# Seven products of 2x2 blocks for eight in the second layer's output sums

## The chip, the cores and the metric

The kernel runs on one NeuronCore of a Trainium2 chip. The metric is the device time of one execution in microseconds (us). The kernel before took 1028.25 us, the median of three runs (1027.79 to 1028.84).

## The reference, cut to what matters

Block-causal attention gives a matrix of 2304 tokens by 512 features; two feed-forward layers follow, the second of which is what the change is about.

```python
def reference(**kwargs):
    ...
    x = np.ascontiguousarray(attn_out.transpose(0, 2, 1, 3)).reshape(B * S, H * D)
    x = _moe_ref(x=x, **moe_kwargs)
    return _moe2_ref(x=x, **moe2_kwargs)

def _moe2_ref(x, w_in, w_out):          # x (2304, 512), w_in (512, 2048), w_out (2048, 512)
    h = x @ w_in
    g = np.maximum(0.01 * h, h)
    return (g @ w_out).astype(np.float32)
```

## The kernel before, in words

**Numbers in two parts.** TensorE multiplies a reduced float format (float32r). So that the result is exact enough, each operand is kept as a high part and a low part (the rest), and each product is three matmuls: high by high, high by low, low by high. The names follow this: `gh` and `gl` are the high and low part of an activation tile, and index 0 or 1 of a weight tile `w` is its high or low part.

**Tiling of the feed-forward layers.** `BLOCKS` (L34) cuts the 2304 tokens of each layer into blocks. In the second layer they are four of 512 tokens and one of 256. The 2048 hidden features are 16 chunks of 128 (`NFC`), the 512 input features four of 128 (`NKC`). `moe_block` (L596) goes over the chunks of a block. The first product of a chunk is 12 matmuls (4 input chunks by 3) into a PSUM bank (L618); a block of 256 tokens puts two chunks into one bank (24 matmuls of 256 columns). ACT and DVE then make the activation: ACT scales the bank by 0.01 (L632), DVE takes the maximum (L634), ACT writes `gh` (L636) and DVE `gl` (L637). The second product has the activation as the stationary operand, 128 tokens of it at a time, and a row of 512 outputs as the moving one (L660): four token groups by three matmuls of 512 columns for a chunk of a 512-token block. It adds up over all 16 chunks in one bank for each token group. At a block's end ACT and DVE copy the banks out (L688, L690) and DMAs write them to `out` (L691).

**Order of the work.** All instructions are entered into a planner (`Plan`) with an estimated cost and a due time (`prio`); a list scheduler then writes out one order for each engine (PE, ACT, DVE, POOL) and for SP's queue, which issues all DMAs. On the chip each engine goes through its own list strictly in turn. In the second layer PE's order is: first product of chunk n+1, second product of chunk n, first product of chunk n+2, and so on. So ACT and DVE have the time of a second product (of the chunk before) and of a first product (of the chunk behind) to make one chunk's activation.

**Buffers.** The weights of the second layer, all 16 chunks in two parts, stay in SBUF (`W`, tiles `w`), converted from 64-bit numbers while the first layer's last block runs (`w_float`, `w_hi`, `w_lo`, L323 being the low parts). The input of a block comes from DRAM (`x2d`) into one of two SBUF areas (`xa`, `xb`; `xbuf`, `moe_load`, L593).

Of the kernel before, what the change touches and what calls it, by code (L numbers as in the profile page):

```python
# [9 lines left out]
F32 = mybir.dt.float32  # L10
# [21 lines left out]


BLOCKS = ([(256 * i, 256) for i in range(5)] + [(1280, 512), (1792, 512)],  # L34
          [(0, 512), (512, 512), (1024, 512), (1536, 512), (2048, 256)])
N_WARM = 10

W1_LO = ("dve", "pool")
# [161 lines left out]
def fused_kernel(ctx, tc, qk, v, w1, w2, out):  # L200
# [3 lines left out]
    def bc(ap):  # L204
        return ap.bitcast(F32)
# [14 lines left out]
    x2d = dr.tile([128, 2, NKC, NTOK], F32, tag="x2d", name="x2d")  # L220
    xa = const.tile([128, 4096], F32R, name="xa")


    def pe(cost, prio, fn, r, w):
        plan.op("PE", cost, prio, fn, r, w)

    def act(cols, prio, fn, r, w, sb=False, extra=0):
        plan.op("ACT", (93 if sb else 51) + 0.833 * cols + extra, prio, fn, r, w)

    def dve(cols, prio, fn, r, w, rate=1.042, fixed=68, port=False):  # L230
        plan.op("DVE", fixed + rate * cols, prio, fn, r, w, port)
# [4 lines left out]
    def dma(nbytes, prio, fn, r, w):  # L236
        plan.op("SP", nbytes / 330.0, prio, fn, r, w)
# [38 lines left out]
    def at(ar, shape, dtype, tag, name, bufs=1):  # L276
        return Buf(plan, (id(ar), tag), bufs,
                   lambda: ar.get().tile(shape, dtype, tag=tag, name=name, bufs=bufs), ar)

    def pt(pool_, shape, dtype, tag, name, bufs):  # L280
        return Buf(plan, (id(pool_), tag), bufs, lambda: pool_.tile(shape, dtype, tag=tag, name=name, bufs=bufs))

    def small(tag, name):
        return pt(st, [128, 4], F32, tag, name, 4)

# [6 lines left out]
    def bank(i):  # L292

        ar = None if i in (4, 5) else ps_d if phase["late"] else ps_c
        return Bank(plan, (i,), lambda: banks[i], ar)

    def xbuf(i):

        if i < 2:
            return Bank(plan, (f"x{i}",), lambda: xa[:, 2048 * i:2048 * i + 2048].rearrange("p (c k t) -> p c k t", c=2, k=NKC))  # L300
        if i == 2:
            return Bank(plan, ("x0", "x1"), lambda: xa.rearrange("p (c k t) -> p c k t", c=2, k=NKC))
        return at(rest, [128, 2, NKC, 512], F32R, "xb", f"xb{i}", 1)


    W = {}
# [274 lines left out]

    def moe_load(layer, i, prio):
        t0, tb = BLOCKS[layer][i]
        x = XB[layer, i] = xbuf(i % 2 if tb < 384 and layer == 0 else (8 - i if i > 4 else i % 2) if layer == 0 else 3 - i % 2)
        if (layer, i) == (0, 0):
            return
        src = (x1d, x2d)[layer]
        name = ("x1d", "x2d")[layer]
        for k in range(NKC):
            have = [q for _, q, wr in plan.regions.get(f"{name}{k}", []) if wr]  # L590
            assert all(any(q[0] <= x < q[1] for q in have) for x in range(t0, t0 + tb, 64)), (layer, i, k)
        for c in range(2):
            dma(512 * tb * 4, prio, lambda c=c: nc.sync.dma_start(bc(x.get()[:, c, :, 0:tb]), src[:, c, :, t0:t0 + tb]),  # L593
                [(f"{name}{k}", (t0, t0 + tb)) for k in range(NKC)], [(x, (4 * c, 4 * c + 4))])
# [98 lines left out]

    EVAC = {"a": ("act", "dve"), "b": ("act", "dve", "act")}
    NP = NKC

# [77 lines left out]
    for fc in range(NFC):  # L776
# [3 lines left out]
        for half in range(2):  # L780
# [2 lines left out]
            src, view = w_float(g - 60, 1, fc, half, hs, WF[fc])  # L783
            w_hi(g - 20, 1, fc, half, src, view, True)
            w_lo(g - 20, 1, fc, half, src, view, True, W2_LO[half])
    for i, (_, tb) in enumerate(BLOCKS[1]):
        if i + 1 < len(BLOCKS[1]):
            moe_load(1, i + 1, t - 20)
        moe_block(1, i, t, 5.5 * tb / 512, hb, [2, 3, 0, 1])
        t += 88 * tb / 512  # L790
    plan.schedule()
    stack["sb"].close()
    for x in ("ps2", "ps"):
# [41 lines left out]
```

## Time and profile before

| what | us |
|---|---|
| median of the three runs | 1028.25 |
| the profiled execution: its time | 1028.8 |
| the profiled execution: span from the first to the last instruction | 1027.0 |
| PE busy / weight loads (PEld) busy | 1003.9 / 832.0 |
| DVE, ACT, POOL busy | 460.4, 443.0, 209.7 |
| second layer, first block (first product of its first chunk to that of the next block) | 617.1 to 706.8 |
| second layer, from there to PE's last matmul | 706.8 to 1023.15 |

The profiled execution's time is 1.8 us longer than its span; that part lies outside the instructions. In the profile, PE is the matmul unit and PEld the loading of stationary operands, which overlaps with it. A matmul's own duration (395 ns at 512 columns) contains waiting in the pipeline, so the pace of PE is read from the distance between starts. A stretch in the chain of waits is written as start, length and what it was; "x12" are twelve instructions in a row. DMA is the share of the core's 16 DMA engines that is busy.

### The profile page before, as it was taken

Reading aid. Unit: us, or ns where it says so; the run is one execution under the profiler, and the core shown is the slowest. Engines: PE = TensorE matmul, PEld = TensorE weight load, DVE = VectorE, ACT = ScalarE, POOL = GpSimd, SP = SyncE. Lnnn points to the kernel's source line nnn. Section 1 sums busy time; section 2 is a strip of 40 time slices with the busy share of each in tenths; the row PEclk is TensorE's granted clock in tenths of the full one; section 3 lists DMA queues with packets and bytes.
Section 4 is the critical chain, followed back from the end, with each engine's and each line's share of the span. In section 5 each row is a group of like instructions: output and inputs, shape, how many; then the busy total and the mean of one; then the engine's idle time right before and its main releaser. Section 6 shows DMA issues by size and latency. Waiting matters only on the chain.

```text
span 1027.0 us, 15314 instructions
## 1 busy us (share of the span) xinstructions
PE 1003.9 (98%) x5908; PEld 832.0 (81%) x5908; DVE 460.4 (45%) x800; ACT 443.0 (43%) x1001; POOL 209.7 (20%) x374
## 2 busy tenths in 40 slices
PE   7798999999999999999999999999999999999998
PEld 4487888888888888988887888888888888888897
DVE  5887755454545444344237994223222222322222
ACT  5776756455555454344346763222222222221221
POOL 6755523233222221111005651000000000000000
PEclk8898999999999999999999999999999999999999
DMA  7765533232342132263034643003000200200010
GB/s 248 218 200 171 176 109 110 92 122 86 117 155 90 48 103 69 93 229 120 1 131 143 198 134 153 1 1 123 0 1 24 99 1 1 82 0 1 1 42 21
DMA packets 51208, 95.35 MB, mean 93 GB/s; under 512 B 4800, under 2 KB 28352, under 8 KB 51136
## 3 DMA queue, kind: packets, MB, share of 16 engines
q1 hardware_dynamic: 51136, 94.39, 28.1%
q8 instruction: 46, 0.75, 0.3%
q14 instruction: 26, 0.21, 0.1%
HBM read 71.83 MB, written 22.54 MB: 92 GB/s over the span
## 4 chain that ended last, share of the span: by engine, by line
PE 93%; DVE 2%; ACT 2%; DMA 1%; POOL 1%; issue 1%; SPq 0%; ACTq 0%; DVEq 0%; POOLq 0%
PE bank L618 40%; PE bank L660 20%; PE bank L653 19%; PE slot L545 5%; PE slot L561 5%; PE slot L485 3%; PE slot L500 1%; DMA wraw<-w 1%; ACT pb L407 1%; POOL pb L418 0%; ACT pa L407 0%; POOL pa L418 0%; ACT bank L347 0%; DVE nmb L400 0%; DVE gl L637 0%
## 5 line engine op out<-in xcount | busy, mean ns | idle before, releaser
L618 PE MATMUL bank<-xa,w 128*128 128x256 f32 (+1 forms) x1536 | 279.7, 330 | 4.9 <-DVE gl L637 4.3
L618 PEld LDWEIGHTS bank<-xa,w 128*128 128x128 f32 x1536 | 230.5, 191 | 43.2 <-issue 11.1
L653 PE MATMUL bank<-gh,w 128*128 128x256 f32 (+1 forms) x896 | 186.1, 318 | 0.0
L660 PE MATMUL bank<-w,gh 128*128 128x512 f32 x576 | 180.8, 395 | 0.0
L618 PE MATMUL bank<-xb,w 128*128 128x512 f32 (+1 forms) x768 | 166.0, 366 | 0.0
L634 DVE TENSOR_TENSOR bank<-bank,g 128x512 f32<-128x512 f32 x72 | 50.4, 700 | 246.9 <-ACT g L632 246.9
L618 PEld LDWEIGHTS bank<-xb,w 128*128 128x128 f32 x768 | 132.1, 188 | 26.4
L653 PEld LDWEIGHTS bank<-gh,w 128*128 128x128 f32 x896 | 134.8, 188 | 22.8 <-issue 11.0
L632 ACT ACTIVATE g<-bank 128x512 f32<-128x512 f32 x72 | 43.1, 598 | 253.0 <-PE bank L618 253.0
L637 DVE TENSOR_TENSOR gl<-bank,gh 128x512 fp32r<-128x512 f32 x144 | 99.2, 689 | 70.3 <-ACT gh L636 69.9
L660 PEld LDWEIGHTS bank<-w,gh 128*128 128x128 f32 x576 | 107.6, 188 | 25.4
L636 ACT ACTIVATE gh<-bank 128x512 fp32r<-128x512 f32 x144 | 86.1, 598 | 91.8 <-DVE bank L634 50.1
L653 PE MATMUL bank<-gl,w 128*128 128x256 f32 (+1 forms) x448 | 114.4, 314 | 0.0
L660 PE MATMUL bank<-w,gl 128*128 128x512 f32 x288 | 113.6, 394 | 0.0
L629 DVE SCALAR_TENSOR_TENSOR bank<-bank,g 128x512 f32<-128x512 f32 x72 | 50.2, 698 | 89.2 <-ACT g L628 89.2
L626 ACT ACTIVATE g<-bank 128x512 f32<-128x512 f32 x72 | 43.1, 598 | 87.5 <-PE bank L618 87.2
L653 PEld LDWEIGHTS bank<-gl,w 128*128 128x128 f32 x448 | 73.2, 188 | 5.8
L418 POOL TENSOR_SCALAR pb<-pb,rsb 128x448 f32<-128x448 f32 (+1 forms) x64 | 45.1, 713 | 113.9 <-DVE rsb L413 112.4
L660 PEld LDWEIGHTS bank<-w,gl 128*128 128x128 f32 x288 | 54.1, 188 | 13.0
L407 ACT ACTIVATE pb<-slot,nmb 128x448 f32<-128x448 f32 (+1 forms) x64 | 43.5, 684 | 34.4 <-DVE nmb L400 33.2
L418 POOL TENSOR_SCALAR pa<-pa,rsa 64x64 f32<-64x64 f32 (+2 forms) x96 | 40.1, 434 | 82.5 <-DVE rsa L413 82.3
L407 ACT ACTIVATE pa<-slot,nma 128x64 f32<-128x64 f32 (+2 forms) x96 | 39.4, 422 | 24.6 <-DVE nma L400 23.3
(77 smaller groups left out, 965.5 us busy)
## 6 DMA issues: line engine op xcount, KB each, us to landing
wraw<-w SPq DMA_DIRECT2D x54, 512.0 KB, 4.2
x2d<-yt SPq DMA_DIRECT2D x36, 256.0 KB, 2.5
qkb<-qk SPq DMA_DIRECT2D x16, 416.0 KB, 3.2
qka<-qk SPq DMA_DIRECT2D x16, 320.0 KB, 3.4
more_raw<-w SPq DMA_DIRECT2D x10, 512.0 KB, 4.9
vb<-v SPq DMA_DIRECT2D x16, 320.0 KB, 2.9
out<-yo SPq DMA_DIRECT2D x18, 256.0 KB, 2.1
x1d<-xpb SPq DMA_DIRECT2D x16, 256.0 KB, 2.9
```

The source lines that it names most:

```text
L407: act(keys, prio, lambda view=view, probs=probs, k=k, i=i: nc.scalar.activation(probs[k](), view()[:, k], AF.Exp, bias=nm.get()[:, i:i + 1 ...
L418: pool(keys, prio, lambda probs=probs, k=k, i=i, rows=rows: nc.gpsimd.tensor_scalar(probs[k]()[0:rows], probs[k]()[0:rows], rs.get()[0:row ...
L545: nc.tensor.transpose(s.get()[:, hd, o:o + 128], pr.get()[:, hd, a:a + 128], ident.get())
L561: nc.tensor.matmul(s.get()[64 * hd:64 * hd + 64, 0, q0:q0 + m], lhsT=vt.get()[:, j, 64 * hd:64 * hd + 64], rhs=pts[i].get()[:, hd, o:o + m ...
L618: nc.tensor.matmul(ps.get()[:, j * tb:(j + 1) * tb], lhsT=win(layer, fc, p, kc), rhs=xt.get()[:, x, kc, 0:tb], start=(k == 0 and kc == 0 a ...
L626: act(nw, pv, lambda ps=ps, gt=gt: nc.scalar.activation(gt.get()[:, 0:nw], ps.get()[:, 0:nw], AF.Relu, bias=0.5, scale=0.5), [ps], [gt])
L629: dve(nw, pv, lambda ps=ps, gt=gt: nc.vector.scalar_tensor_tensor(ps.get()[:, 0:nw], ps.get()[:, 0:nw], 1.0, gt.get()[:, 0:nw], op0=ALU.ma ...
L634: dve(nw, pv, lambda ps=ps, gt=gt: nc.vector.tensor_tensor(ps.get()[:, 0:nw], ps.get()[:, 0:nw], gt.get()[:, 0:nw], op=ALU.max), [ps, gt], ...
L636: act(nw, pv, lambda ps=ps, gh=gh: nc.scalar.activation(gh.get()[:, 0:nw], ps.get()[:, 0:nw], AF.Copy), [ps], [gh])
L637: dve(nw, pv, lambda ps=ps, gh=gh, gl=gl: nc.vector.tensor_tensor(gl.get()[:, 0:nw], ps.get()[:, 0:nw], bc(gh.get()[:, 0:nw]), op=ALU.subt ...
L653: nc.tensor.matmul(y[o].get()[:, e * tb:(e + 1) * tb], lhsT=wout(0, fc, p)[:, ec * 128:ec * 128 + 128], rhs=x.get()[:, j * tb:(j + 1) * tb ...
L660: nc.tensor.matmul(y[o].get(), lhsT=x.get()[:, j * tb + o * 128:j * tb + o * 128 + 128], rhs=wout(1, fc, p), start=(fc == 0 and k == 0), s ...
```

## The change

From the second block of the second layer on, tokens are taken in blocks of 256, and two hidden chunks (a pair, 8 pairs) are worked on at a time. The second product of a pair is then a product of 2x2 blocks: on one side two token groups of 128 by two chunks, on the other two chunks by two halves of 256 outputs. The plain way takes eight block products (24 matmuls of 256 columns with the three parts); the changed kernel takes seven (21), with sums and differences of blocks on both sides and seven sums at the end (the scheme of Strassen and Winograd).

- `combine_weights` makes the weight side once for each pair: three combined blocks, which go in two parts to DRAM (`tsd`) because SBUF has no room, and a fourth that is written over the second half of the even chunk's `w`. This is planned beside the first block (still `moe_block`, 512 tokens).
- `moe_seven` takes the place of `moe_block` for the seven blocks of 256. It loads a pair's three combined blocks from `tsd` into one half of `xb` (L773), makes the activation into `e` (L776, L777), four sums and differences of 128 columns (L781), and the high and low parts of all (`ea` L779, L783; `gh`, `gl` L785, L786). The second product is four groups of matmuls on four banks (L816).
- At a block's end one ACT copy and seven DVE sums of 256 columns (L828, L835, L837) make the outputs in place of the copies.

The diff, cut to its core:

```diff
 BLOCKS = ([(256 * i, 256) for i in range(5)] + [(1280, 512), (1792, 512)],
-          [(0, 512), (512, 512), (1024, 512), (1536, 512), (2048, 256)])
+          [(0, 512)] + [(256 * i, 256) for i in range(2, 9)])
...
+    def combine_weights(p, prio):
...
+        for i, w in enumerate((wa, wb)):
+            dve(512, prio, lambda i=i, w=w: nc.vector.tensor_tensor(
+                b(2 * i, 2), bc(w.get()[:, 0, 512:1024]), bc(w.get()[:, 1, 512:1024]), op=ALU.add),
...
+            dve(256, prio, lambda o=o, x=x, y=y: nc.vector.tensor_tensor(t(o), x(), y(), op=ALU.subtract), r, [(tt, (o, o + 1))], port=True)
+        act(256, prio, lambda: nc.scalar.activation(wa.get()[:, 0, 768:1024], t(3), AF.Copy), [(tt, (3, 4))], [(wa, (2, 3))], sb=True)
...
+        act(768, prio, lambda: nc.scalar.activation(b(0, 3).bitcast(F32R), t(0, 3), AF.Copy), [(tt, (0, 3))], [(bb, (0, 3))], sb=True)
...
+            dma(393216, prio, lambda c=c, v=v: nc.sync.dma_start(tsd[:, p, c], v(0, 3)), [(x, (0, 3))], [("tsd", (2 * p + c, 2 * p + c + 1))])
+
+    def moe_seven(i, p0, dp, hbanks, ybanks):
...
+                for j in range(2):
+                    fc = 2 * p + j
+                    for k, (c, x) in enumerate(((0, 0), (1, 0), (0, 1))):
...
+                                nc.tensor.matmul(ps.get()[:, j * 256:(j + 1) * 256], lhsT=win(1, fc, c, kc),
...
+                dma(786432, pr - 4, lambda p=p, tt=tt: nc.sync.dma_start(bc(tt.get()), tsd[:, p].rearrange("p c (i n) -> p c i n", i=3)),
+                    [("tsd", (2 * p, 2 * p + 2))], [tt])
+                pv = pr - 8
+                act(512, pv, lambda ps=ps, e=e: nc.scalar.activation(e.get()[:, 512:1024], ps.get(), AF.Copy, scale=0.01), [ps], [(e, (4, 8))])
+                dve(512, pv, lambda ps=ps, e=e: nc.vector.tensor_tensor(e.get()[:, 0:512], ps.get(), e.get()[:, 512:1024], op=ALU.max),
+                    [ps, (e, (4, 8))], [(e, (0, 4))])
+                act(384, pv, lambda ah=ah, e=e: nc.scalar.activation(ah(0), e.get()[:, 128:512], AF.Copy), [(e, (1, 4))], [(ea, (0, 1))], sb=True)
+                for o, a, b, op in ((4, 0, 2, ALU.add), (5, 4, 1, ALU.subtract), (6, 1, 0, ALU.subtract), (7, 3, 5, ALU.subtract)):
+                    dve(128, pv, lambda at_=at_, o=o, a=a, b=b, op=op: nc.vector.tensor_tensor(at_(o), at_(a), at_(b), op=op),
...
+                act(512, pv, lambda sh=sh, e=e: nc.scalar.activation(sh.get(), e.get()[:, 512:1024], AF.Copy), [(e, (4, 8))], [sh], sb=True)
...
+                for o, prods in enumerate((((av(0), bv(0, 0)), (av(2), bv(1, 0))),
+                                           ((sv(2), tv(2)), (sv(3), tv(3))),
+                                           ((av(1), tv(4)), (sv(1), t1)),
+                                           ((sv(4), bv(1, 1)),))):
...
+                            for k, (ca, cb_) in enumerate(((0, 0), (0, 1), (1, 0))):
+                                nc.tensor.matmul(m[o].get()[:, 256 * z:256 * z + 256], lhsT=a(ca), rhs=b(cb_),
...
-    for i, (_, tb) in enumerate(BLOCKS[1]):
+    moe_load(1, 1, t - 20)
+    moe_block(1, 0, t, 5.5, hb, [2, 3, 0, 1])
+    for p in range(NFC // 2):
+        combine_weights(p, t + 11 * p + 12)
+    t += 88
+    yb = [6, 7, 2, 3, 0, 1]
+    for i in range(1, len(BLOCKS[1])):
         if i + 1 < len(BLOCKS[1]):
             moe_load(1, i + 1, t - 20)
-        moe_block(1, i, t, 5.5 * tb / 512, hb, [2, 3, 0, 1])
-        t += 88 * tb / 512
+        moe_seven(i, t, 5.4, hb, yb)
+        t += 43.2
```

How the rows of three engines change (lines of the changed kernel stand four or more below those of the kernel before):

PE, the middle of a block of the second layer. `w_4` to `w_13` are weight chunks, `gh_1_3` the activation of block 1, chunk 3 (before) or pair 4 (changed). Before, two chunks of 512 tokens:

```order
L618 MATMUL bank_77<-xa,w_4_5956 128x512 x12
L660 MATMUL bank_5133<-w_3_5905,gh_1_3_7120 128x512 [waits Activation_49]
L660 MATMUL bank_5133<-w_3_5905,gh_1_3_7120 128x512
L660 MATMUL bank_5133<-w_3_5905,gl_1_3_7125 128x512 [waits DVE_49]
L660 MATMUL bank_5134<-w_3_5905,gh_1_3_7120 128x512 x2
L660 MATMUL bank_5134<-w_3_5905,gl_1_3_7125 128x512
...
L618 MATMUL bank_78<-xa,w_5_6008 128x512 x12
```

Now one pair of 256 tokens:

```order
L751 MATMUL bank_78<-xa,w_10_6268 128x256 x12
L751 MATMUL bank_78<-xa,w_11_6320 128x256 x12
L816 MATMUL bank_5138<-w_8_6164,ea_1_4_7392 128x256 [waits Activation_49]
L816 MATMUL bank_5138<-w_8_6164,ea_1_4_7392 128x256
L816 MATMUL bank_5138<-w_8_6164,ea_1_4_7392 128x256 [waits DVE_49]
L816 MATMUL bank_5138<-w_9_6216,ea_1_4_7392 128x256 x3
L816 MATMUL bank_5139<-xb,gh_1_4_7405 128x256 [waits DMAHW6_49,Activation_49]
L816 MATMUL bank_5139<-xb,gh_1_4_7405 128x256
L816 MATMUL bank_5139<-xb,gl_1_4_7415 128x256 [waits DVE_49]
L816 MATMUL bank_5139<-xb,gh_1_4_7405 128x256 x2
...
L816 MATMUL bank_5134<-xb,ea_1_4_7392 128x256 x3
```

The first product of pair 5 stands ahead of the second product of pair 4, as before with chunks; new is a wait for a DMA (the pair's blocks in `xb`) at the seventh matmul.

DVE in the same place, one pair of the changed kernel (before: L634 and L637 for each chunk, nothing else):

```order
L777 TENSOR_TENSOR e_1_4_7376<-bank_77,e_1_4_7376 128x512 [waits Activation_49]
L781 TENSOR_TENSOR e_1_4_7376<-e_1_4_7376 128x128 [waits DVE_49]
L781 TENSOR_TENSOR e_1_4_7376<-e_1_4_7376 128x128
L781 TENSOR_TENSOR e_1_4_7376<-e_1_4_7376 128x128 [waits DVE_49]
L783 TENSOR_TENSOR ea_1_4_7392<-e_1_4_7376,ea_1_4_7392 128x384 [waits Activation_49]
L781 TENSOR_TENSOR e_1_4_7376<-e_1_4_7376 128x128 [waits DVE_49]
L786 TENSOR_TENSOR gl_1_4_7415<-e_1_4_7376,gh_1_4_7405 128x512 [waits Activation_49]
```

Seven instructions for a pair of 256 tokens stand where four stood for two chunks of 512.

SP's queue from the last two pair loads of block 1 to the first two of block 2 (`xb<-tsd` are the pair loads, `xa<-x2d` the input of block 3):

```order
L773 DMA xb<-tsd 128x1536 [waits DMAHW6_49,DMAHW0_49,PE_49]
L773 DMA xb<-tsd 128x1536 [waits DMAHW7_49,DMAHW1_49,PE_49]
L597 DMA xa<-x2d 128x4x256 [waits DMAHW2_49,PE_49]
L597 DMA xa<-x2d 128x4x256 [waits DMAHW3_49,PE_49]
L773 DMA xb<-tsd 128x1536 [waits DMAHW0_49,PE_49]
L773 DMA xb<-tsd 128x1536 [waits DMAHW1_49,PE_49]
L840 DMA out<-ys_1_1_7671 128x512 [waits DVE_49]
```

Eight loads of a pair's blocks for each block of tokens are new; the two input loads stand ahead of the next block's first pair load.

## Rows read from the trace of the kernel before

**Rows 1.** Page: busy time, share, instructions; granted clock in 40 slices, tenths.
```profile
PE 1003.9 (98%) x5908; PEld 832.0 (81%) x5908; DVE 460.4 (45%) x800; ACT 443.0 (43%) x1001; POOL 209.7 (20%) x374
...
PEclk8898999999999999999999999999999999999999
```

**Rows 2.** Busy time by stretch: PE, PEld, DVE, ACT, POOL, granted clock, DMA share, GB/s.
```profile
617.10:706.70 89.60, 89.60 (x386) 72.16 (x385) 26.70 (x39) 23.62 (x41) 2.59 (x2) 1.00 0.12 45
...
885.69:975.10 89.41, 89.41 (x386) 72.06 (x386) 23.60 (x34) 20.32 (x34) 0.00 (x0) 1.00 0.05 20
...
975.13:1014.72 39.59, 39.59 (x254) 35.86 (x254) 11.09 (x16) 9.56 (x16) 0.00 (x0) 1.00 0.07 28
```

**Rows 3.** Chain of waits, second layer: start, length, what.
```profile
706.76 2.80 PE bank L618 x12
...
885.69 2.80 PE bank L618 x12
...
975.13 2.88 PE bank L618 x24
...
1014.72 2.84 PE bank L618 x24
...
1017.56 5.59 PE bank L660 x24
```

**Rows 4.** Busy time in two stretches of the first layer, columns as in Rows 2.
```profile
560.00:617.00 57.00, 57.00 (x246) 45.88 (x245) 53.96 (x72) 41.04 (x70) 34.53 (x30) 1.00 0.54 173
426.92:438.29 11.37, 11.37 (x97) 11.37 (x97) 2.78 (x5) 3.66 (x6) 0.00 (x0) 1.00 0.67 219
```

**Rows 5.** Instructions in order of time, end of the second layer's first block.
```profile
703.80 0.63 PE L660 MATMUL bank<-w,gh 128*128 128x512 f32 x2
...
704.06 0.60 ACT L632 ACTIVATE g<-bank 128x512 f32<-128x512 f32 x1 [3.63 <-PE bank L618]
...
704.69 0.70 DVE L634 TENSOR_TENSOR bank<-bank,g 128x512 f32<-128x512 f32 x1 [3.54 <-ACT g L632]
...
705.42 0.60 ACT L636 ACTIVATE gh<-bank 128x512 fp32r<-128x512 f32 x1 [0.77 <-DVE bank L634]
...
706.05 0.69 DVE L637 TENSOR_TENSOR gl<-bank,gh 128x512 fp32r<-128x512 f32 x1 [0.67 <-ACT gh L636]
```

**Rows 6.** Groups by shape, ACT and DVE: busy us, mean ns, idle before.
```profile
L628 ACT ACTIVATE g<-g 128x512 f32<-128x512 f32 x72 | 45.5, 632 | 1.6
...
L576 DVE TENSOR_TENSOR xpb<-slot,xpb 128x256 fp32r<-128x256 f32 x16 | 6.8, 422 | 17.4 <-ACT xpb L574 17.4
...
L574 ACT ACTIVATE xpb<-slot 128x256 fp32r<-128x256 f32 x16 | 6.1, 381 | 15.9 <-PE slot L561 15.8
...
L576 DVE TENSOR_TENSOR xpa<-slot,xpa 128x64 fp32r<-128x64 f32 x4 | 0.8, 212 | 0.0
```

**Rows 7.** DMA issues, 300 to 1027 us: KB each, median us to landing.
```profile
wraw<-w SPq DMA_DIRECT2D x32, 512.0 KB, 4.2
...
xb<-x2d SPq DMA_DIRECT2D x4, 1024.0 KB, 6.3
```

**Rows 8.** Instructions in order of time as the second layer starts: DVE and PE.
```profile
612.09 0.68 DVE L637 TENSOR_TENSOR gl<-bank,gh 128x512 fp32r<-128x512 f32 x1
...
612.69 0.68 DVE L360 SCALAR_TENSOR_TENSOR wpre<-bank,wsg 128x512 int32<-128x512 int32 x1
...
613.28 1.52 DVE L323 TENSOR_TENSOR w<-wpre,w 128x512 fp32r<-128x512 f32 x1
615.88 0.70 DVE L629 SCALAR_TENSOR_TENSOR bank<-bank,g 128x512 f32<-128x512 f32 x1 [1.07 <-ACT g L628]
...
617.24 0.69 DVE L637 TENSOR_TENSOR gl<-bank,gh 128x512 fp32r<-128x512 f32 x1 [0.66 <-ACT gh L636]
...
619.92 0.63 PE L653 MATMUL bank<-gh,w 128*128 128x512 f32 x2
```

**Rows 9.** The last copy of an output bank, in order of time.
```profile
1023.18 0.69 DVE L690 COPY yo<-bank 128x512 f32<-128x512 f32 x1 [2.83 <-PE bank L660]
```

More of the change, by code (lines that the diff above doesn't have):

```diff
@@ L221, in fused_kernel @@
     xa = const.tile([128, 4096], F32R, name="xa")
+    tsd = dr.tile([128, NFC // 2, 2, 768], F32, tag="tsd", name="tsd")
     def pe(cost, prio, fn, r, w):
@@ L281, in pt @@
         return Buf(plan, (id(pool_), tag), bufs, lambda: pool_.tile(shape, dtype, tag=tag, name=name, bufs=bufs))
+    xb = at(rest, [128, 4096], F32R, "xb", "xb")
     def small(tag, name):
@@ L302, in xbuf @@
             return Bank(plan, ("x0", "x1"), lambda: xa.rearrange("p (c k t) -> p c k t", c=2, k=NKC))
-        return at(rest, [128, 2, NKC, 512], F32R, "xb", f"xb{i}", 1)
+        return Bank(plan, ("xb0", "xb1"), lambda: xb.get().rearrange("p (c k t) -> p c k t", c=2, k=NKC), rest)
     W = {}
@@ L583, in moe_load @@
         t0, tb = BLOCKS[layer][i]
-        x = XB[layer, i] = xbuf(i % 2 if tb < 384 and layer == 0 else (8 - i if i > 4 else i % 2) if layer == 0 else 3 - i % 2)
+        x = XB[layer, i] = xbuf(i % 2 if tb < 384 else (8 - i if i > 4 else i % 2) if layer == 0 else 3 - i % 2)
         if (layer, i) == (0, 0):
@@ L692, in moe_block, with b, t @@
                 out[t0 + o * 128:t0 + o * 128 + 128, :], ys.get()), [ys], [])
+    def combine_weights(p, prio):
+        wa, wb = W[1, 2 * p], W[1, 2 * p + 1]
+        bb, tt = (pt(cv, [128, 512], I64, "wraw", f"{x}{p}", 3) for x in ("bb", "tt"))
+        def b(i, n=1):
+            return bb.get().bitcast(F32)[:, 256 * i:256 * i + 256 * n]
+        def t(i, n=1):
+            return tt.get().bitcast(F32)[:, 256 * i:256 * i + 256 * n]
+        for i, w in enumerate((wa, wb)):
+            dve(512, prio, lambda i=i, w=w: nc.vector.tensor_tensor(
+                b(2 * i, 2), bc(w.get()[:, 0, 512:1024]), bc(w.get()[:, 1, 512:1024]), op=ALU.add),
+                [(w, (2, 4))], [(bb, (2 * i, 2 * i + 2))], port=True)
+        for o, x, y, r in ((3, lambda: b(1), lambda: b(0), [(bb, (0, 2))]), (1, lambda: b(3), lambda: b(1), [(bb, (1, 4))]),
+                           (0, lambda: b(3), lambda: t(3), [(bb, (3, 4)), (tt, (3, 4))]),
+                           (2, lambda: t(0), lambda: b(2), [(bb, (2, 3)), (tt, (0, 1))])):
+            dve(256, prio, lambda o=o, x=x, y=y: nc.vector.tensor_tensor(t(o), x(), y(), op=ALU.subtract), r, [(tt, (o, o + 1))], port=True)
+        act(256, prio, lambda: nc.scalar.activation(wa.get()[:, 0, 768:1024], t(3), AF.Copy), [(tt, (3, 4))], [(wa, (2, 3))], sb=True)
+        dve(256, prio, lambda: nc.vector.tensor_tensor(wa.get()[:, 1, 768:1024], t(3), bc(wa.get()[:, 0, 768:1024]), op=ALU.subtract),
+            [(tt, (3, 4)), (wa, (2, 3))], [(wa, (3, 4))], port=True)
+        act(768, prio, lambda: nc.scalar.activation(b(0, 3).bitcast(F32R), t(0, 3), AF.Copy), [(tt, (0, 3))], [(bb, (0, 3))], sb=True)
+        dve(768, prio, lambda: nc.vector.tensor_tensor(t(0, 3).bitcast(F32R), t(0, 3), b(0, 3), op=ALU.subtract),
+            [(bb, (0, 3))], [(tt, (0, 3))], port=True)
+        for c, x, v in ((0, bb, b), (1, tt, t)):
+            dma(393216, prio, lambda c=c, v=v: nc.sync.dma_start(tsd[:, p, c], v(0, 3)), [(x, (0, 3))], [("tsd", (2 * p + c, 2 * p + c + 1))])
```

73 lines of the change are left out of this document (added).

## The prediction

> **What bounds the kernel now.** I read the page's busy times first, then the busy time by stretch, then the chain of waits through the second layer, then single instructions. PE is busy for 98% of the span [rows 1]. Its granted clock is 9 tenths or more from the fifth slice on and 1.00 in every stretch of the second layer, the upper of its two levels, 2.4 GHz [rows 1, 2]. In the second layer PE has no idle time at all: 89.41 of 89.41 us in one block, with DVE busy for 23.60 and ACT for 20.32 [rows 2]. The chain of waits names nothing but PE from the second block's start to its last matmul [rows 3]. So time goes only if PE's matmuls become fewer or shorter, and it comes back only if something makes PE wait.
>
> **PE's own work, the main term.** From 885.69 to 975.13 us PE does one block of 512 tokens, 192 matmuls for each product and 384 in all, each of 512 columns [rows 3]: 89.44/384 = 0.2329 us for one. From 975.13 to 1014.72 it does seven rounds of the block of 256: 24 matmuls of 256 columns and 12 of 512. That is 39.59 us; less 84 x 0.2329 = 19.56 it leaves 20.03 for 168, so 0.1192 us for one of 256 columns.
>
> Before, from 706.76 (first product of the second block's first chunk) to 1017.56 + 5.59 = 1023.15 [rows 3], PE spends 316.4 us. The count gives the same: 12 matmuls left over from the first block, 3 x 384 and 96 make 1260 of 512 columns (293.5 us), and 192 of 256 (22.9 us). After the change there are the same 12 and, for seven blocks of eight pairs, 24 + 21 = 45 of 256 columns: 2520 x 0.1192 = 300.4, and 2.8 for the 12: 303.2 us. **PE saves 13.2 us.**
>
> Two things work against each other in that. Seven for eight saves 24 of 192 narrow matmuls in each block of 256. But two narrow matmuls (0.2384) cost more than a wide one (0.2329), so the first product of three blocks pays 576 x 0.0055 = 3.2 us, which the sum holds. In the Trainium skill, TensorE: Matmul & The Clock Gate, section Back-to-back issue gap, a matmul of N columns is N/2.4 + 2.5 ns behind the last, 215.8 and 109.2 here; by that the sum would be -15.1 us instead of -13.2, a time inside the range below. The rows show 232.9 and 119.2, and they decide.
>
> Is 0.1192 right when every matmul is narrow? The nearest row is a stretch of the first layer in which both products have 256 columns: 96 matmuls (the row counts one at the edge too) in 11.37 us, 0.1184 each, with the DMA engines 67% busy beside them [rows 4]. The bounds are 0.1184 (2.0 us less) and 2.88/24 = 0.120 [rows 3] (2.0 more); I take 0.1192.
>
> **ACT's and DVE's chain for a pair.** What PE waits for must be done while PE does 21 matmuls of the pair before and 24 of the pair behind; the low part is first read by the ninth matmul after those: 53 x 0.1192 = 6.32 us. In the chain of before, PE leaves the bank at 703.80, ACT starts 0.26 later, DVE's maximum 0.89 later, and a hand-over costs about 0.03 [rows 5]. The new chain: ACT L776 and DVE L777 as before, to 1.59. Then DVE's sums of 128 columns, for which there is no row; between 212 ns (64 columns) and 422 (256) [rows 6] I take 0.28. Three of them end at 2.45 and cover ACT's L779 (384 columns, about 0.51 between 0.381 and 0.632). L783 (384, about 0.55) ends at 3.00, the fourth sum at 3.28, ACT L785 (0.63) at 3.94, DVE L786 (0.69) at 4.66. Slack is 1.66 us; at 0.42 for a sum it is still 1.1, at 0.21 more. DVE is busy for 3.1 of 5.36 us a pair, ACT for 1.8. **Cost: nothing**, by the cover of two products of PE. At a block's end seven DVE sums of 256 columns (0.42 each, 2.9 us) share that time; they stand behind the next pair's L777 in DVE's order, and most stand behind its L786 too.
>
> **The pair loads.** A load of 768 KB has no row: 512 KB take 4.2 us to landing, 1024 KB 6.3 [rows 7], so about 5.2. A half of `xb` is free after 15 of 21 matmuls of a pair's second product and read again at the seventh matmul two pairs later: (90 - 15 + 6) x 0.1192 = 9.66 us. That covers it, at both bounds. Behind the two input loads of the next block (1024 KB) in SP's queue it is tightest: all one after the other 11.5 us, and PE needs them 96 matmuls (11.4 us) after the input area came free. So 0 to 0.2 us for each of six blocks; nothing by the row of both in flight together: a block moves 6.3 + 1.05 + 0.5 MB in 42.9 us, 183 GB/s, and 173 to 219 GB/s ran beside a busy PE before, without a slower pace [rows 4].
>
> **Making the combined blocks.** For a pair DVE gets two sums of 512 (0.69), five of 256 (0.42) and one of 768 columns (about 0.96), 4.4 us; ACT 0.38 and about 0.88. Eight pairs add 35.6 us to DVE's 26.70 and 10.1 to ACT's 23.62 in a first block of 89.60 [rows 2]; its chain is shorter than the one above and PE's cover longer, so nothing there. Tightest is the start: the first pair's sums run in the first layer's last two chunks, where DVE was nearly full. Ahead of the last chunk's L637, eight instructions (4.7 us, or 4.0 as starts lie 0.60 apart where durations are 0.68) meet idle time of 1.07 and 0.66 and the 2.46 us from 617.93 to the third matmul after 619.92 (620.39) [rows 8]: 4.2 us. Even, so 0; the upper bound is 2 us, if L323 and the new sums hold each other up with POOL (L323 took 1.52 there instead of 0.69).
>
> **The end.** Before, the last copy starts at 1023.18 and lasts 0.69 [rows 9], 3.13 us ahead of the span's end; PE had ended at 1023.15. Now the last outputs come out of the seven sums, which can start when the first bank is full. They take 4.0 us (starts 0.33 apart) to 4.4 from the start of PE's last 2.5, so they end 1.5 to 1.9 after PE and not 0.7: 0.8 to 1.2 us more, or 0.5 if the narrow sums are quicker. I take **+0.8**.
>
> **Sum.** -13.2 + 0.8 = -12.4 us. The profiled execution's 1028.8 becomes 1016.4; the median of the runs is 0.55 lower, so **1015.9 us**.
>
> **Rivals.**
> - *The chain outgrows its cover (slower).* If DVE's operations from SBUF to SBUF ran as L323 did in rows 8, 2.2 times as long, the three sums, L783, the fourth sum and L786 would add some 2.9 us: the chain ends at 7.5, PE waits 1.2 us for each of 56 pairs, 67 us, about 1083. It decides from a chain of 6.55 us on (12.4/56 = 0.22 us of wait). Against it: POOL, which had work beside that L323, does nothing in these blocks [rows 2]. 5%.
> - *The pair loads set the pace (slower).* If a load takes the 11.5 us of the two in turn every time, two pairs take that and the 1.1 us in which the half is read, 6.3 us a pair and not 5.36: +53 us, about 1069. Against it: 9.66 us against 5.2. 2%.
> - *The weight loads set the pace (slower).* PEld is 81% busy in blocks of 512 columns (72.06 of 89.41) and all the time in the narrow stretch (11.37 of 11.37) [rows 2, 4]. At the mixed stretch's 35.86/254 = 0.141 us for a load, 2520 x 0.022 = +55, about 1071. By Perfetto Trace Analysis of the Trainium skill, section Identifying the Most-Contended Engine, it is the share of weight loads, not of matmuls, that tells TensorE's headroom; by that rule there would be none left. But the same narrow row has a pace of 0.1184. 1%.
> - *Waits at the edges (a smaller gain).* Seven block starts at about 1 us each, with the start's 2: 1022 to 1026. For it: the two tight places above; against: PE never waited at such an edge before. 5%.
> - *No change* within 2 us, by several of these at once: 2%. That the matmuls don't become fewer is excluded by PE's order.
>
> **How the numbers follow.** The forecast has 85%. Its range: down by 2.0 (pace 0.1184) and 0.3 (end) to 1013.5; up by 2.0 (pace), 1 (input loads), 2 (start) and 0.4 (end), with a little of the edges, to 1022. About 0.2%, 2 us, is what a measurement of this kernel can tell from no change. Faster: 85 + 5 = 90%; same 2%; slower 5 + 2 + 1 = 8%.
>
> **What would show it.** In the changed profile PE should have no idle time from the first block to the last matmul, with pieces of 45 matmuls in 5.36 us and blocks of 42.9 us; DVE's wait for ACT and ACT's for PE should hold nearly all their idle time; the pair loads should land in 5 to 6 us; the last DVE sum should end 1.5 to 1.9 us after PE. It is wrong if PE has waits in front of L816 for DVE, ACT or a DMA, or if a narrow matmul costs more than 0.120 us.

## The result and the profile after

The changed kernel takes 1013.99 us (median of 4 runs, 1013.50 to 1014.71), the kernel before 1028.02 in the same comparison: a ratio of 0.9859, with a 95% interval of 0.9847 to 0.9871. The forecast was 1015.9, in a range of 1013.5 to 1022.0. The profiled execution took 1013.73 us, with a span of 1011.9.

The page of the changed kernel: busy time, granted clock, one group of instructions, and the pair loads (KB each, us to landing).

```profile
PE 986.1 (97%) x6988; PEld 870.6 (86%) x6988; DVE 582.3 (58%) x1186; ACT 481.4 (48%) x1073; POOL 208.9 (21%) x374
...
PEclk9899999999999999999999999999999999999999
...
L781 DVE TENSOR_TENSOR e<-e 128x128 f32<-128x128 f32 x224 | 54.9, 286 | 1.7
...
xb<-tsd SPq DMA_DIRECT2D x55, 768.0 KB, 4.3
```

PE executes 1080 matmuls more than before [rows 1], most of them half as wide, and is busy for 17.8 us less; DVE has 121.9 us more and is still far from full.

The busy time of three stretches of the changed kernel: PE, PEld, DVE, ACT, POOL, granted clock, DMA share, GB/s.

```profile
616.37:705.84 89.47, 89.47 (x386) 72.07 (x386) 55.47 (x97) 32.12 (x55) 3.38 (x2) 1.00 0.33 123
...
705.84:1006.96 301.12, 301.12 (x2532) 300.36 (x2531) 170.96 (x441) 102.53 (x178) 0.00 (x0) 1.00 0.54 176
...
754.10:796.70 42.60, 42.60 (x362) 42.60 (x362) 24.28 (x64) 14.43 (x25) 0.00 (x0) 1.00 0.58 186
```

The first row is the second layer's first block, beside which the combined blocks are made (the first pair's sums mostly ahead of it, in the first layer): DVE's busy time doubles against the first of [rows 2] and PE's time does not move. The second row is all that follows to the last matmul. PE has no idle time in it, the clock stays at the upper level, and PEld is busy for 300.36 of 301.12 us. The third row is one block of 256: 42.60 us.

The chain of waits of the changed kernel from the second block on: start, length, what.

```profile
705.84 2.84 PE bank L751 x24
...
716.81 2.84 PE bank L751 x24
719.65 2.49 PE bank L816 x21
...
999.48 5.71 PE bank L816 x48
1005.19 0.02 issue
```

A round of 24 and 21 matmuls takes 2.84 + 2.49 = 5.33 us, 0.1184 for one. Before, this stretch ran from 706.76 to the end of the last matmul's record at 1023.14; now it runs from 705.84 to 1006.96, as in the windows. **PE's part is 15.3 us shorter.**

The changed kernel's instructions in order of time, one pair of the second block (start, length, engine and line; in brackets the idle time before, and what ended it).

```profile
740.80 0.87 PE L816 MATMUL bank<-w,ea 128*128 128x256 f32 x6
740.99 0.60 ACT L776 ACTIVATE e<-bank 128x512 f32<-128x512 f32 x1 [1.88 <-PE bank L751]
741.51 0.39 PE L816 MATMUL bank<-xb,gh 128*128 128x256 f32 x2
741.62 0.69 DVE L777 TENSOR_TENSOR e<-bank,e 128x512 f32<-128x512 f32 x1 [1.78 <-ACT e L776]
...
742.21 0.52 PE L816 MATMUL bank<-xb,ea 128*128 128x256 f32 x3
742.35 0.69 DVE L781 TENSOR_TENSOR e<-e 128x128 f32<-128x128 f32 x3
...
742.76 0.32 SPq L773 DMA_DIRECT2D xb<-tsd  x1
...
743.81 0.63 ACT L785 ACTIVATE gh<-e 128x512 fp32r<-128x512 f32 x1 [0.93 <-DVE e L781]
744.47 0.69 DVE L786 TENSOR_TENSOR gl<-e,gh 128x512 fp32r<-128x512 f32 x1 [0.76 <-ACT gh L785]
...
747.07 0.28 PE L816 MATMUL bank<-xb,gl 128*128 128x256 f32 x1
```

PE leaves the first product's bank at 740.80, and the chain over ACT and DVE ends at 744.47 + 0.69 = 745.16, 4.36 us later; PE reads the low part first at 747.07, 6.27 us later. The slack is 1.9 us. The load into the half of `xb` that PE stopped reading at 742.73 is issued at 742.76 and lands 4.3 us later, at about 747.1; PE wants that half two rounds after 741.51, at 752.17, so here the slack is 5.1 us.

The end of the changed kernel, in order of time.

```profile
1006.68 0.28 PE L816 MATMUL bank<-w,gl 128*128 128x256 f32 x1
1007.09 0.41 DVE L835 TENSOR_TENSOR ys<-yu,bank 128x256 f32<-128x256 f32 x1
1007.42 0.75 DVE L837 TENSOR_TENSOR ys<-bank,yu 128x256 f32<-128x256 f32 x2
1007.86 0.81 SPq L840 DMA_DIRECT2D out<-ys  x2
```

PE's last record ends at 1006.96, the last sum at 1008.17, and the span at 1011.9: 4.94 us behind PE. Before it was 1027.0 - 1023.14 = 3.86, so the end costs 1.1 us more.

The spans differ by 15.1 us: 15.3 of PE's part and 0.9 ahead of the second layer (it begins at 616.37 and not at 617.28), less 1.1 at the end. The 0.9 can't be put down to the change: the medians differ by 14.0, near to the 14.2 of the other two, and in the last experiment below the second layer of one and the same kernel starts 4.07 us apart in two runs.

### The profile page after: what moved, and what is told of

The parts are those of the page before. It is cut to its first block, busy times and chain, and to the rows that moved or that the text cites. A ratio compares the mean times of both kernels' runs of the same rounds, so it can differ in the third digit from the quotient of the medians.

```text
span 1011.9 us, 18123 instructions
## 1 busy us (share of the span) xinstructions
PE 986.1 (97%) x6988; PEld 870.6 (86%) x6988; DVE 582.3 (58%) x1186; ACT 481.4 (48%) x1073; POOL 208.9 (21%) x374
## 4 chain that ended last, share of the span: by engine, by line
PE 93%; DVE 3%; ACT 2%; issue 1%; DMA 1%; POOL 0%; SPq 0%; DVEq 0%; ACTq 0%
PE bank L622 24%; PE bank L657 19%; PE bank L751 16%; PE bank L816 14%; PE slot L549 5%; PE slot L565 5%; PE bank L664 4%; PE slot L489 3%; PE slot L504 1%; ACT pb L411 1%; DMA wraw<-w 1%; DVE nmb L404 0%; ACT pa L411 0%; DVE more_sg L354 0%; DVE w L327 0%
## 5 line engine op out<-in xcount | busy, mean ns | idle before, releaser
L622 PE MATMUL bank<-xa,w 128*128 128x256 f32 (+1 forms) x1152 | 182.6, 306 | 4.3 <-DVE gl L641 4.3
L622 PEld LDWEIGHTS bank<-xa,w 128*128 128x128 f32 x1152 | 156.2, 189 | 25.4 <-issue 11.2
L751 PE MATMUL bank<-xa,w 128*128 128x256 f32 x1344 | 167.9, 281 | 0.0
L751 PEld LDWEIGHTS bank<-xa,w 128*128 128x128 f32 x1344 | 163.1, 188 | 0.2
L622 PE MATMUL bank<-xb,w 128*128 128x512 f32 x384 | 94.7, 394 | 0.0
L777 DVE TENSOR_TENSOR e<-bank,e 128x512 f32<-128x512 f32 x56 | 38.7, 691 | 88.2 <-ACT e L776 87.9
L622 PEld LDWEIGHTS bank<-xb,w 128*128 128x128 f32 x384 | 72.1, 188 | 17.0
L630 ACT ACTIVATE g<-bank 128x512 f32<-128x512 f32 x72 | 43.1, 599 | 83.9 <-PE bank L622 83.6
L776 ACT ACTIVATE e<-bank 128x512 f32<-128x512 f32 x56 | 33.4, 597 | 102.7 <-PE bank L751 102.7
L641 DVE TENSOR_TENSOR gl<-bank,gh 128x512 fp32r<-128x512 f32 x88 | 60.5, 688 | 32.7 <-ACT gh L640 32.3
L785 ACT ACTIVATE gh<-e 128x512 fp32r<-128x512 f32 x56 | 35.4, 632 | 52.7 <-DVE e L781 52.6
L786 DVE TENSOR_TENSOR gl<-e,gh 128x512 fp32r<-128x512 f32 x56 | 38.8, 692 | 37.2 <-ACT gh L785 37.2
L781 DVE TENSOR_TENSOR e<-e 128x128 f32<-128x128 f32 x224 | 54.9, 286 | 1.7
```

Source lines behind the costliest of these rows:

```text
L622: nc.tensor.matmul(ps.get()[:, j * tb:(j + 1) * tb], lhsT=win(layer, fc, p, kc), rhs=xt.get()[:, x, kc, 0:tb], start=(k == 0 and kc == 0 a ...
L641: dve(nw, pv, lambda ps=ps, gh=gh, gl=gl: nc.vector.tensor_tensor(gl.get()[:, 0:nw], ps.get()[:, 0:nw], bc(gh.get()[:, 0:nw]), op=ALU.subt ...
L751: nc.tensor.matmul(ps.get()[:, j * 256:(j + 1) * 256], lhsT=win(1, fc, c, kc), rhs=xt.get()[:, x, kc, 0:256], start=(k == 0 and kc == 0 an ...
L781: dve(128, pv, lambda at_=at_, o=o, a=a, b=b, op=op: nc.vector.tensor_tensor(at_(o), at_(a), at_(b), op=op), [(e, (a, a + 1)), (e, (b, b + ...
```

## Experiments

In each trace I read two things besides the time: the *mark*, where the second layer's first second product starts (a piece of six matmuls in the chain; 625.68 us before, 624.76 after), and the end of PE's last product or of the span. What lies between is free of the first layer, and does not show what is done for the second layer ahead of the mark. The marks in the two chains of waits (start, length, what), before and then changed:

```profile
625.68 1.38 PE bank L660 x6
```
```profile
624.76 1.38 PE bank L664 x6
```

Before, from the mark to the end of PE's last product it is 397.47 us; in the changed kernel 382.20, and 387.14 to the end of the span.

### What PE's time is made of

**Blocks of 256, eight products.** From the changed kernel:

```
-    for p in range(NFC // 2):
-        combine_weights(p, t + 11 * p + 12)
...
-        moe_seven(i, t, 5.4, hb, yb)
-        t += 43.2
+        moe_block(1, i, t, 2.75, hb, [2, 3] if i % 2 else [0, 1])
+        t += 44
```

> The changed kernel with its blocks of 256 tokens but with the plain second product (eight block products, as 12 matmuls of 512 columns for a pair), no combined blocks, no pair loads. PE has 7 x (192 narrow + 96 wide) matmuls and 12 wide ones. If a narrow matmul costs 0.1192 us, as the mixed block of before gave, PE needs 319.5 us against 316.3 before: +3.2, about 1031.2. If a narrow one costs 0.1184 and the rest of the 0.1192 belongs to changing between widths, the mixed stretch still reads 0.1192 here and the time is the same 1031.2; at 0.1184 in the mix too it would be +2.1, about 1030.1. In either case it is slower than before: cutting the blocks alone gains nothing.

Measured: 1030.48 us, ratio 1.0024 (1.0015 to 1.0034). From the mark at 624.55 PE takes to 1024.29, 399.74 us: +2.27, next to the lower of the two expectations. In its chain of waits (start, length, what) every round is like these two:

```profile
1010.19 2.84 PE bank L622 x24
1013.03 2.80 PE bank L664 x12
```

So a narrow matmul among wide ones takes 2.84/24 = 0.1184 us too. The 2.88 of [rows 3] belongs to the block of before whose input lies in `xb`, and there only to every second piece; here every input is in `xa`, and no piece is longer than 2.84. What makes those pieces 0.04 longer is not settled: the experiment below has such pieces with another operand there.

**The second product narrow as well** (in the blocks of 256 tokens), still eight; added to the edit above:

```
-                                    nc.tensor.matmul(y[o].get(),
...
+                                    for z in range(0, 512, 512 if tb > 256 else 256):
+                                        nz = 512 if tb > 256 else 256
+                                        nc.tensor.matmul(y[o].get()[:, z:z + nz],
...
+                                                         rhs=wout(1, fc, p)[:, z:z + nz],
```

> As eight_mixed, but the second product's matmuls have 256 columns too (24 for a pair in place of 21 in the changed kernel): eight products at the same width as the seven. If PE's pace is all that counts, PE needs 2688 x 0.1184 + 2.8 = 321.1 us, 4.7 more than before: about 1032.7, and 168 x 0.1184 = 19.9 us more PE time than the changed kernel, less about 1.1 us for the shorter end. If a narrow matmul costs 0.1192 everywhere, about 1034.9. Were the changed kernel's gain from something else than the number of matmuls, this would lie nearer to 1014 than 19 us above it.

Measured: 1035.05 us, ratio 1.0065 (1.0042 to 1.0087). From the mark at 625.62 to 1029.05 it is 403.43 us, +5.96 against before. Its chain of waits:

```profile
1006.21 2.88 PE bank L666 x24
1009.09 2.84 PE bank L622 x24
1011.93 2.85 PE bank L666 x24
```

The second product's pieces alternate between 2.88 and 2.85. With these two kernels the 15.3 us split up: blocks of 256 cost 2.3, the second product in narrow matmuls 3.7 more (5.96 - 2.27), and seven for eight gives 403.43 - 382.20 = 21.2 back. Of that, 56 pairs x 3 matmuls x 0.1184 are 19.9; the rest is pace: in the changed kernel 21 matmuls of the second product take 2.49 us, which is 2.85 for 24, and here the mean is 2.865.

### What lies beside PE's work

**Making the combined blocks, nothing else.** The kernel before, with `tsd`, `combine_weights` and its calls beside the first block; the blocks of tokens and `moe_block` stay.

```
+        if i == 0:
+            for p in range(NFC // 2):
+                combine_weights(p, t + 11 * p + 12)
```

> The kernel before with the combined weight blocks made and stored beside the second layer's first block, and nothing else: the second products stay plain (from the second block on they use the even chunks' overwritten halves, so the output is another one). My theory, that DVE, ACT and the stores are hidden: no change, 1028 within 1 us, PE without idle time between 617 us and the end. The rival, that the first layer's last chunks or the first block wait for the added DVE work: up to 2 us more, with PE waits for gl between 606 and 640 us.

Measured: 1028.19 us, ratio 1.0000 (0.9988 to 1.0012); from the mark at 624.06 to 1021.54 it is 397.48 us against 397.47 before. The stretch of the first block, columns as above:

```profile
617.00:706.70 89.70, 89.70 (x387) 72.23 (x386) 54.68 (x96) 31.57 (x55) 3.30 (x2) 1.00 0.31 115
```

DVE has 28.0 us more and ACT 8.0 more than in the first of [rows 2], and PE is never idle. The first pair's sums lie ahead of the mark; there PE has no wait from 600 us on, and the whole times agree within 1.2 us. So no cost of the making is seen.

**No pair loads.** The changed kernel, with a block that is already in SBUF in place of the loaded ones:

```
-                dma(786432, pr - 4, lambda p=p, tt=tt: nc.sync.dma_start(...), [("tsd", ...)], [tt])
...
-                    return lambda c: tt.get()[:, c, i - 2]
+                    return bv(0, 0)
```

> The changed kernel without the loads of the combined blocks: the matmuls that would read them take a resident weight block instead (so the output is another one); the blocks are still made and stored. If the loads are hidden and do not slow PE: the same 1014 within 1 us, 45 matmuls in 5.33 us. If they cost anything, by a wait or by slowing the matmuls that read while DMA writes: faster by that, 0.1 us a pair being 5.6 us.

Measured: 1015.19 us, ratio 0.9867 (0.9849 to 0.9885). From the mark at 626.27 to 1007.80 it is 381.53 us, where the changed kernel has 1005.19 - 624.76 = 380.43: without the loads it is 1.1 us longer, not shorter. Its chain of waits:

```profile
988.49 2.52 PE bank L814 x21
...
993.85 2.49 PE bank L814 x21
```

Every second piece of the second product takes 2.52 and not 2.49; 28 x 0.03 is most of the 1.1. The other pieces take 2.49 us with and without the loads, and in the changed kernel PE never waits for one. So the loads cost nothing, at a rate of 176 GB/s beside a busy PE. That every second piece is slower by one per cent is seen here again, now with another operand in the second product; why is not explained.

**How far the loads are from setting the pace.** Two kernels were to leave one half of `xb` unused:

```
-                tt = Bank(plan, (f"xb{p % 2}",), lambda p=p: xb.get()[:, p % 2 * 2048:p % 2 * 2048 + 1536]...
+                tt = Bank(plan, ("xb0",), lambda p=p: xb.get()[:, 0:1536]...
```

> The changed kernel with one half of the area for the pair loads in place of two, so a pair's load starts only when the pair before has been read. A pair then takes at least the load (4.3 us), its issue and hand-overs (about 0.7) and the 1.1 us in which PE reads it, 6.1 us and not 5.33: about 43 us more, 1045 to 1065, with PE waiting for the DMA. If the second half is not needed: 1014.

Measured: 1204.97 us. The run says nothing on the question: the load of a pair is entered into the planner before the reads of the pair before, so with one half the planner puts each load ahead of those reads, and PE reads the next pair's blocks in their place. The second try enters the load behind those reads:

> The pair loads go into one half of xb only, and a pair's load is now entered behind the reads of the pair before. If the second half is what hides a load: the load can start after the 15th of a pair's 21 matmuls and is needed at the seventh of the next pair, 36 to 37 matmuls later, 4.3 us; the loads took 4.3 us from issue to landing in the changed kernel, and with hand-overs of 0.3 to 0.8 us PE waits 0.3 to 0.8 us in each of some 50 pairs, 15 to 40 us in all: 1029 to 1054 us, and the waits stand in front of L816 and name the load. If the loads are faster than that when nothing is beside them, or the second half was never needed, there is no wait and 1013 to 1015 us.

Measured: 1165.59 us, and again not for the reason expected. PE's and ACT's waits in its second layer (engine, line, waited for: us in total, times, longest):

```profile
PE bank L807 <- ACT ea L770: 47.6, 47, 1.0
...
PE bank L807 <- DMA xb<-tsd: 6.0, 4, 3.7
...
ACT gh L776 <- PE bank L807: 264.2, 45, 7.1
```

Only 6.0 us are waits for a load. With one half, the planner writes PE's list with a first product one pair further ahead; then `gh`, which has two buffers, is free only when PE has read it, and ACT's L776 waits for PE in 45 pairs. What a single half costs in the old order was not measured.

The third kernel leaves the lists of PE, ACT and DVE as they are and issues each load twice:

```
-                dma(786432, pr - 4, lambda p=p, tt=tt: nc.sync.dma_start(...), ...)
+                def load(p=p, tt=tt):
+                    for _ in range(2):
+                        nc.sync.dma_start(...)
+
+                dma(786432, pr - 4, load, ...)
```

> Every pair load is issued twice, the same 768 KB into the same half of xb, the second behind the first; the order on PE, ACT and DVE is the changed kernel's. A load took 4.3 us from issue to landing there, so two behind each other take some 8.6 us, and a half is free for 9.66 us by the prediction's count (81 matmuls; 9.59 at 0.1184). If that count is right, the doubled load just fits where nothing else is in the queue: 1014 to 1016 us, with waits of some tenths at the block edges, where two input loads stand before it. If the loads' margin is smaller than counted, PE waits in front of L816 for xb<-tsd in every pair: 1 us of it in 55 pairs would give 1069. If the two overlap in the queues, they land together in 5 to 6 us and the time is the changed kernel's, 1013 to 1015.

Measured: 1109.51 us, ratio 1.0795 (1.0766 to 1.0824): far slower than any of the three cases expected. Waits of PE and of SP's queue from the second block on, a part of its chain of waits (start, length, what), and PE's instructions around one wait:

```profile
PE bank L819 <- DMA xb<-tsd: 64.3, 44, 8.3
...
SPq L775 <- DMA xb<-tsd: 315.6, 55, 8.3
```
```profile
774.48 6.90 DMA xb<-tsd
781.40 0.33 SPq L775
781.82 6.05 DMA xb<-tsd
```
```profile
771.08 0.76 PE L819 MATMUL bank<-xb,gh 128*128 128x256 f32 x2 [3.63 <-DMA xb<-tsd]
...
771.86 0.63 PE L819 MATMUL bank<-xb,gh 128*128 128x256 f32 x2
...
779.26 0.40 PE L819 MATMUL bank<-xb,gh 128*128 128x256 f32 x2
...
785.85 0.47 PE L819 MATMUL bank<-xb,gh 128*128 128x256 f32 x2 [1.44 <-DMA xb<-tsd]
...
786.28 0.40 PE L819 MATMUL bank<-xb,gh 128*128 128x256 f32 x2
```

The expectation looked at the half of `xb` alone. But the second load writes where the first does, so it waits in SP's queue until the first has landed, and all that stands behind it there waits as well: the next pair's first load starts only then, beside the second load of this pair, and two in flight land in 6.05 and 6.90 us here instead of 4.3. A step of the chain, landing and issue, is one pair: from 774.48 to 781.82 it is 7.3 us, where PE needs 5.33. The mean of all is (1109.5 - 1014.0)/55 = 1.74 us more a pair, 7.07. So the rival that the loads set the pace is a real mechanism, and it is SP's order that calls it up.

### The chain over ACT and DVE

Copies of `e` onto itself on ACT, between L777 and L779, lengthen every pair's chain; two in one kernel, four in the other:

```
+                for _ in range(2):
+                    plan.op("ACT", 1, pv, lambda e=e: nc.scalar.activation(e.get()[:, 0:512], e.get()[:, 0:512], AF.Copy), ...)
```

> The changed kernel with two more ACT copies of the 512 columns onto themselves between the maximum and the sums, in each pair's chain; PE's and DVE's orders are unchanged. Each lengthens the chain by about 0.66 us. In the changed kernel the low parts end 4.36 us after PE leaves the bank and are read 6.27 after it, slack about 1.9 less a hand-over. Theory: 1.3 us more fits, no change, 1014 to 1015. If the chain had no slack: 56 x 1.3 = 73 us more.

Measured: 1016.6 us (one run). The second layer started late in it: from the mark at 627.25 to the end of the span at 1014.8 it is 387.55 us, 0.4 more than in the changed kernel, and PE waited once, for 0.2 us. A chain of about 4.36 + 2 x 0.66 = 5.7 us is still covered.

> As chain_2 with four copies, 2.6 us more: the low parts would end about 7.0 us after PE leaves the bank, 0.7 to 1.0 after PE wants them. Theory: PE waits that long for gl or gh in nearly each of 56 pairs, 40 to 55 us more, about 1054 to 1069. If PE could run ahead over it, less than 10 us more.

Measured: 1060.94 us (one run). From the mark at 624.91 to the end of the span at 1059.1 it is 434.19 us: +47.05, within the expectation. One pair in its chain of waits:

```profile
800.51 0.69 DVE gl L788
801.21 0.61 DVE e L777
...
801.84 0.64 ACT e L780
...
804.50 0.70 DVE e L783 x3
...
805.90 0.64 ACT gh L787
...
806.56 0.69 DVE gl L788
```

PE is not in it: from L788 to L788 it is 6.05 us on ACT and DVE alone, 0.72 above PE's round, and 56 x 0.72 = 40 of the 47 us. Some 5 more come at the six block edges, where DVE makes the end sums as well and two rounds take 6.27 and 6.70 us. The limit shows in another form than the prediction gave it. In DVE's list the next pair's L777 stands behind this pair's L788, and starts here as soon as that ends; so the way from L777 to the end of L788 (L786 in the changed kernel) must also fit into one round of 5.33 us. In the changed kernel it takes from 741.62 to 745.16, 3.54 us, which leaves 1.8. ACT has such a round too, from L776 to the end of `gh`: from 740.99 to 744.44, 3.45 us.

### The first block in 256 too

```
-          [(0, 512)] + [(256 * i, 256) for i in range(2, 9)])
+          [(256 * i, 256) for i in range(9)])
...
-        combine_weights(p, t + 11 * p + 12)
-    t += 88
+        combine_weights(p, t + 5.4 * p + 6)
+    t += 44
```

The first block, now of 256, goes by eight products and covers the making of the combined blocks, and eight blocks go by seven.

> The changed kernel with the first block of the second layer cut to 256 tokens too (plain there), so that eight blocks and not seven take the seven products; the combined blocks are made at twice the pace. PE's work falls by 89.4 - 45.2 - 42.6 = 1.6 us: about 1012.4 if the faster making is hidden. If DVE, with some 36 us for the blocks and 13 for the chain in a block of 45 us, comes late: PE waits of 1 to 4 us in the first 60 us of the second layer, 1013 to 1016.

Measured: 1012.0 us (median of 5), ratio 0.9847 (0.9834 to 0.9861). From the start of the second layer's first product at 615.04 to 1002.07, where the chain leaves PE, it is 387.03 us; in the changed kernel, from 616.37 to 1005.19, 388.82: 1.79 less. Both were run once more, on one chip:

> All eight blocks of the second layer in 256 tokens and by seven products. By the theory that PE's matmuls are the whole time, the first block saves 48 of 768 narrow matmuls' worth against blocks of 256 by eight and pays for halves: 384 matmuls of 512 columns at 0.2329 (89.4 us) become 2 x 360 of 256 at 0.1184 (85.2), but the first of its two blocks can't use the sums before they are made and keeps eight products, 2 x 384 - 24 at the most; measured once, 1.8 us less in the second layer. Expected: 1.5 to 2.0 us below the changed kernel on the same chip. By the rival (the first run's start of the second layer was early by chance, and nothing is gained) the two agree within 0.5 us.

> The changed kernel once more, beside the version with the first block in 256 tokens, on one chip. Expected by its own earlier times: 1012 to 1015.5 us, ratio to the kernel before 0.985 to 0.988. The theory that the spread between runs lies in the first layer expects that from the start of the second layer's first second product to the end of the span it takes 387.1 us within 0.4, wherever the second layer starts; if the spread lies in the second layer too, that stretch differs by as much as the total.

Measured: 1012.92 us, ratio 0.9850 (0.9833 to 0.9868), and 1013.68 for the changed kernel, ratio 0.9860 (0.9840 to 0.9879). The medians are 0.8 us apart and the intervals overlap; the traces are clearer. The version's chain of waits this time:

```profile
619.11 2.84 PE bank L622 x24
...
1000.42 5.71 PE bank L816 x48
1006.13 0.02 issue
```

That is 387.02 us, to 0.01 what it was, though the second layer began 4.07 us later than in the first run. The changed kernel has 388.82 again, from 616.34 to 1005.16, and 387.17 from its mark at 624.73 to the end of the span (387.14 before). So in these four traces the second layer takes the same time whenever it starts, its gain of 1.8 us is real, and the 4 us between the two traces of this version are made in the first layer. By its second layer this version beats both kernels; in whole times the 0.8 us are not clear of the spread.

## Why the prediction was right

1. **What bounds the kernel.** As forecast, PE has no idle time from the first block to its last matmul, and the chain of waits names only PE there.
2. **PE's work: the count right, the pace mis-sized.** The forecast was -13.2 us at 0.1192 us for a narrow matmul; measured were -15.3 at 0.1184. The step that was off is "I take 0.1192" instead of the row of 0.1184 [rows 4], which had narrow matmuls in both products, as the changed kernel has. The 0.1192 came out of a block [rows 3] in which every second piece takes 2.88, and that does not come back where the inputs lie in `xa`. 2520 x 0.0008 = 2.0 is nearly all of the difference; the measured time is close to the lower end of the range, 1013.5, which was made of this bound and 0.3 of the end. The prediction names the wide matmuls of the first product that become two narrow ones; the same holds for the second product, 672 x 0.0055 = 3.7 us, which its sum of 2520 contains and its text does not name. The experiments measured 2.3 for the first product and 3.7 for the second. By the figures of the Trainium skill (TensorE: Matmul & The Clock Gate, Back-to-back issue gap), which the page calls those of an isolated matmul and not of a stream of weight loads and matmuls, the sum is -15.1 as an estimate, close to what came out. But its 109.2 and 215.8 ns both lie 8% below the measured 118.4 and 232.9, before and after the change alike, and a difference of two sums hides that.
3. **The chain.** Forecast 4.66 us in a cover of 6.32, measured 4.36 in 6.27. The sum of 128 columns, with no row before, was put at 0.28 and took 0.286; three in a row take 0.69 in all, since their starts lie closer than their durations. That the cost is nothing was shown by the two and four copies: 1.3 us more cost 0.4, 2.6 us more cost 47. The limit is there, and the prediction's 6.55 was near to it, but it missed the second form of it, the round on DVE and ACT themselves.
4. **The pair loads.** Forecast 5.2 us to landing in a window of 9.66, measured 4.3 (the slowest 6.9) in 9.4 (742.76 to 752.17). Cost nothing, as taken. The rival's price (1069) was in its mechanism right and too low: with every load held in turn behind another it was 1109.
5. **The combined blocks.** No cost seen: 397.48 against 397.47, and no wait of PE at the tight start, where the sum took an even balance. DVE has 28.8 us more in the first block (55.47 against 26.70) and not 35.6, as the first pair's sums lie mostly ahead of it.
6. **The end.** Forecast +0.8, measured +1.1, inside the bounds. The sums end 1.4 us after PE's last matmul (1006.80 by the pace), a little under the forecast 1.5 to 1.9; behind them it is 3.73 us to the end of the span and not 3.13. The two outputs are issued closer together than before (L840: 1007.9 and 1008.3, before 1023.1 and 1023.9), and the slower one lands in 2.3 us where both took 2.0. That this is the reason was not tested; for those 0.6 us the sum had no term.
7. **The rivals.** None came. Weight loads are busy for 300.36 of 301.12 us and PE keeps the pace of 0.1184 with no wait, so a full PEld is no price of its own here; whether it is what sets 0.1184 stays open.

With the measured terms, -15.3 + 1.1 = -14.2, the median of 1028.25 becomes 1014.1; 1013.99 was measured.

## What to carry to other kernels

Where one engine is never idle, count its instructions and take their pace from the stretch whose mix of shapes and operands is nearest to the new one; in a sum over 2520 instructions, 0.8 ns of each decides 2 us. Work that an added algorithm gives to other engines and queues was free here up to a limit that has two forms: the delay from release to use, and the round of each engine or queue on its own; both are read in one pair of the timeline. When a few microseconds are looked for, compare from a mark behind the part that varies from run to run, not spans.

## What was not expected of the hardware

- **A wait of PE can cost more than its length.** In the kernel with doubled loads, the matmuls behind a wait of 3.63 us (771.08) lie 0.21 us apart instead of 0.118: two in a row take 0.63 us at 771.86 and 0.40 at 779.26, which is the lower level of the clock, 1.2 GHz. The granted clock is 0.50 from 771.05 to 774.20 us and 1.00 again from 778.18 to 781.00. Behind a wait of 1.44 us (785.85) they keep the upper. The granted clock of that kernel's stretch from 750 to 850 us is 0.93, where the changed kernel has 1.00, and with one half of `xb` the mean of the whole run fell to 0.924. The kernel with doubled loads lies 95.5 us above the changed one, and 66.9 of them are counted as waits of PE; the slower matmuls are part of the rest, which was not split up. With the four copies PE's waits are 0.6 us at most, and the clock stays at 0.990.
- **Every second piece of narrow matmuls can take 0.03 to 0.04 us longer**: the kernel before shows it in the first product, two experiments in the second (2.88 and 2.85, 2.52 and 2.49). It changes with the operands that are read; the cause was not looked for.
- **Two loads of 768 KB in flight at once** land in 5.5 us (median, from 720 to 1000 us) instead of 4.3, at 245 to 256 GB/s.
